# Splitting the next group's x on VectorE alone, one part per slot, with other engines for the first group's copies and another list of steps

## The chip, the cores and the metric

The kernel runs on one core of a Trainium2 chip. The metric is the device time of one execution in microseconds (us). The kernel before was run three times: median 1244.37 us, from 1243.97 to 1244.62. One more execution was taken by the hardware profiler; it took 1244.99 us.

## The reference

The inputs are x (2048 tokens of 512 values), weights of an attention with 32 query heads of 16 values that share one key head and one value head, weights of a gated feed-forward network with 1376 hidden columns, and a gate vector.

```python
g = _sigmoid((x * gate_w).sum(-1, keepdims=True))
a = _A_ref(x, A_wq, A_wk, A_wv, A_wo)          # softmax(q k^T / 4) v, then wo
b = _B_ref(x, B_w_gate, B_w_up, B_w_down)      # (gelu(x w_gate) * (x w_up)) w_down
return g * a + (1 - g) * b
```

## The kernel before, in words

**Number format.** The projections and the network are computed in three passes: each float32 operand is split into a high part (rounded to the matmul's fp32r type by a cast, L198) and a low part (the remainder by a subtraction, L199), and high x high, high x low and low x high are added up in PSUM. `split` makes the two parts; `split_part` does it for one staged piece of 128x512 and then calls `fetch`, which issues the DMA of a later piece on SyncE's queue. Four staging tiles `st` hold the pieces, three of them fetched ahead. A transfer into a tile waits until the subtraction that last read it is over. Normally the cast runs on VectorE and the subtraction on GpSimd.

**Order of the work.** The tokens stand in four groups of 512. A prologue goes through the groups in the order 1, 2, 3, 0: keys, values, one block of the network, and the queries (four blocks b of L258 for each group), which go to DRAM. For the last of these, group 0, x is also copied into the layout of the main loop (`xd`, 16 copies of 64x1024, L495 to L505 of the kernel), four copies after each block b. Then come the maximum of the bounds (`pairmax`, L510 to L514, which needs the bound of the last block, L284), the shift row, and the first scores.

**The main loop** is written out as a list, `PLAN`, and played by `play`. One line is one job on TensorE: a gate job (`f:` with 24 steps F of two matmuls on 64 rows each, L550), two down jobs after every three or four gate jobs (L561; 18 or 24 F), or an output job (`w:`). H takes the two PSUM banks z and y for the job, R ends it. S and Z are scores of the attention (L796, two matmuls and an exp on ScalarE, L800, of 1024 columns); Z takes the third of the score banks, which is the one that z uses. V adds one tile of probabilities x values (L867, 8 matmuls). T and the scores that follow move the steps of the gelu on: copy out of z (L587), two operations (L590, L591), a tanh on ScalarE (L594), two operations (L597, L598; the second reads y), and a split of the result (L602, L603).

**Slots.** After every third F of a job one piece of waiting work is put on VectorE's queue (`slot`): first from `todo` (splits of weights and of x), else from `bg` (the normalization of the attention: reciprocals L833 and others). In the first half of a job with two terms lists (`pair_mm`), `todo` is passed over in late slots. A down job's result is added to `acc` from its banks at its end (L665, L667): VectorE's queue is in order, so this waits for whatever was put there before, and the next job's H, or a Z, needs the banks. When a chunk of attention ends, its bank is copied out (L810, L821).

**Change of group.** After the last gate job of a group, `queue_x` puts the next group's x, eight parts, into `todo`, two to an item: the first split normally, the second wholly on VectorE. They are done in the two down jobs that follow. There are three such changes.

Of the kernel before, what the change touches and what calls it, by code (L numbers as in the profile page):

```python
# [20 lines left out]
S = 2048  # L21
# [98 lines left out]
def mix_kernel(ctx, tc, xT, xD, wq, wo, wf, out):  # L120
# [257 lines left out]

    def queue_x(tg):
        ps = x_parts(tg)  # L380

        def two(a, b):
            split_part(a)
            split_part(b, nc.vector)

        todo.extend(lambda i=i: two(ps[i], ps[i + 1]) for i in range(0, len(ps), 2))
# [37 lines left out]
    def first_gelu(tg):  # L424
# [17 lines left out]
        def halves():  # L442
# [7 lines left out]
            else:  # L450
                for a, h in enumerate((hh, hl)):
                    nc.sync.dma_start(hs[tg - 1, a], h.bitcast(F32))

        return inner, tanh, outer, halves

    def v_rows(tg):
        nc.scalar.copy(vt[32 * tg : 32 * tg + 32], first[tg][1][RF:P])

    hold = []
    supply.pop(0)  # L460
    d_tiles(0)
    fetch()
    for ti, tg in enumerate(order):
        xh, xl = xs[tg]
# [90 lines left out]
    def pair_mm(z, y, X, Y):  # L555
        for half in range(2):
            for q in range(len(X)):
# [15 lines left out]
                if q % EVERY == EVERY - 1 and (half == 0 or q + 4 <= len(X)):  # L573
                    slot(half == 1 or q + 6 <= len(X))
# [414 lines left out]
```

## Time and profile before

| what | before |
|---|---|
| median of three runs | 1244.37 us |
| the profiled execution, its time | 1244.99 us |
| its span, first to last instruction | 1243.2 us |
| mean granted TensorE clock | 0.993 |
| TensorE busy | 1226.1 us (99%) |
| ScalarE busy | 1031.0 us (83%) |
| VectorE busy | 600.2 us (48%) |
| GpSimd busy | 229.2 us (18%) |
| DMA, mean rate | 62 GB/s |

The engines are called PE (TensorE's matmuls), PEld (its weight loads), DVE (VectorE), ACT (ScalarE), POOL (GpSimd) and SP (SyncE, which issues most DMAs; SPq is its queue). L199 is line 199 of the kernel. A row of a timeline gives the start in us from the span's start, the duration in us, the engine, line and operation, output <- input by the program's names, and how many such instructions are merged; in brackets stands how long the engine was idle before, and what ended that. A group of concurrent matmuls overlaps, so durations of single matmuls don't add up. The mean clock of a window is 1.00 where TensorE's full clock was granted throughout.

### The profile page before, as it was taken

What the parts mean: (1) busy time and instruction counts of PE and PEld (TensorE: products, weight loads), DVE (VectorE), ACT (ScalarE), POOL (GpSimd) and SP (SyncE); (2) the same over time, 40 slices, a digit from 0 to 9 for tenths busy, and PEclk for the clock granted to TensorE, in tenths of its full rate; (3) what the DMA queues carried; (4) which work ended last, traced back from release to release, by engine and by line L of the source; (5) the groups of instructions that cost most, each with busy time, mean ns of one, the idle gap of its engine ahead of it and who ended that gap; (6) DMA issues with size and microseconds to landing.
All of it is one profiled execution on the core that took longest, in us unless ns stands there. A gap on an engine that the chain in (4) does not pass through costs nothing.

```text
span 1243.2 us, 23284 instructions
## 1 busy us (share of the span) xinstructions
PE 1226.1 (99%) x9742; PEld 680.0 (55%) x9742; DVE 600.2 (48%) x856; ACT 1031.0 (83%) x1131; POOL 229.2 (18%) x196
## 2 busy tenths in 40 slices
PE   9999999999999999999999999999989999999998
PEld 7865455545455555555555555554545554555555
DVE  7884166345545145533736244533755332471543
ACT  5458998887699888898888789888869898899883
POOL 5531033021121012101222011201231000120200
PEclk9999999999899999999999999999989999999999
DMA  8641031012221111102231111201231110110100
GB/s 330 212 130 49 1 95 53 23 58 64 68 75 48 32 48 57 40 23 65 69 103 45 48 40 49 57 23 40 69 93 55 56 32 25 51 56 24 40 1 34
DMA packets 41563, 77.03 MB, mean 62 GB/s; under 512 B 5680, under 2 KB 5936, under 8 KB 41456
## 3 DMA queue, kind: packets, MB, share of 16 engines
q1 hardware_dynamic: 40912, 74.47, 19.5%
q8 instruction: 77, 1.26, 0.4%
q0 software_dynamic: 256, 0.79, 0.2%
q14 instruction: 30, 0.25, 0.1%
q10 hardware_dynamic: 288, 0.26, 0.1%
HBM read 60.56 MB, written 14.94 MB: 61 GB/s over the span
## 4 chain that ended last, share of the span: by engine, by line
PE 87%; DVE 5%; ACT 1%; DMA 0%; issue 0%; ACTq 0%; DVEq 0%
PE acc L867 36%; PE s L796 22%; PE z L550 15%; PE z L561 8%; PE y L561 4%; PE y L550 2%; DVE xl L199 1%; PE wos L538 1%; DVE xh L198 0%; ACT p L800 0%; DMA st<-xD 0%; DVE n L830 0%; DVE nz L827 0%; DVE hl L603 0%; PE u L538 0%; DVE acc L677 0%
## 5 line engine op out<-in xcount | busy, mean ns | idle before, releaser
L800 ACT ACTIVATE p<-s 128x1024 f32<-128x1024 f32 x1024 | 972.7, 1026 | 146.6 <-PE s L796 145.2
L867 PE MATMUL acc<-p,v 128*32 128x512 f32 x4096 | 487.7, 601 | 0.0
L796 PE MATMUL s<-Q,kp 51*128 51x512 f32 x2048 | 385.4, 416 | 8.1 <-DVE acc L667 7.5
L796 PEld LDWEIGHTS s<-Q,kp 51*128 51x128 f32 x2048 | 186.6, 185 | 216.7 <-ACT p L800 110.2
L199 POOL TENSOR_TENSOR gl<-st,gh 128x512 fp32r<-128x512 f32 x80 | 112.7, 1428 | 862.7 <-PE s L796 439.2
L867 PEld LDWEIGHTS acc<-p,v 128*32 128x32 f32 x4096 | 115.8, 109 | 254.2 <-issue 243.7
L550 PE MATMUL y<-xh,gh 64*128 64x512 f32 x312 | 123.1, 395 | 1.5 <-DVE gs L598 1.5
L550 PE MATMUL z<-xh,gh 64*128 64x512 f32 x312 | 123.2, 395 | 0.0
L550 PE MATMUL z<-xl,gh 64*128 64x512 f32 x312 | 122.3, 392 | 0.0
L587 DVE COPY gs<-z 128x512 f32<-128x512 f32 x39 | 26.4, 676 | 198.6 <-PE y L550 189.8
L550 PE MATMUL y<-xl,gh 64*128 64x512 f32 x312 | 122.2, 392 | 0.0
L550 PE MATMUL y<-xh,gl 64*128 64x512 f32 x312 | 121.8, 390 | 0.0
L550 PE MATMUL z<-xh,gl 64*128 64x512 f32 x312 | 121.8, 390 | 0.0
L561 PE MATMUL y<-dh,hh 64*128 64x512 f32 x176 | 71.2, 405 | 0.2 <-DVE acc L667 0.2
L561 PE MATMUL z<-dh,hh 64*128 64x512 f32 x176 | 71.2, 405 | 0.0
L199 POOL TENSOR_TENSOR dl<-st,dh 128x512 fp32r<-128x512 f32 x44 | 64.7, 1473 | 24.4 <-DVE dh L198 20.9
L561 PE MATMUL y<-dl,hh 64*128 64x512 f32 x176 | 69.1, 393 | 0.0
L561 PE MATMUL z<-dl,hh 64*128 64x512 f32 x176 | 69.1, 392 | 0.0
L561 PE MATMUL z<-dh,hl 64*128 64x512 f32 x176 | 68.9, 391 | 0.0
L561 PE MATMUL y<-dh,hl 64*128 64x512 f32 x176 | 68.8, 391 | 0.0
L550 PEld LDWEIGHTS z<-xl,gh 64*128 64x128 f32 x312 | 58.4, 187 | 9.8
L550 PEld LDWEIGHTS z<-xh,gl 64*128 64x128 f32 x312 | 57.5, 184 | 10.6
(180 smaller groups left out, 1529.6 us busy)
## 6 DMA issues: line engine op xcount, KB each, us to landing
st<-wf SPq DMA_DIRECT2D x125, 256.0 KB
scr<-q SPq DMA_DIRECT2D x16, 512.0 KB
Q<-scr SPq DMA_DIRECT2D x64, 128.0 KB
st<-xD SPq DMA_DIRECT2D x24, 256.0 KB
Q<-scr SPq DMA_DIRECT2D x64, 64.0 KB
out<-acc SPq DMA_DIRECT2D x16, 256.0 KB
xr<-xT SPq DMA_DIRECT2D x6, 512.0 KB
xr<-xT SPq DMA_DIRECT2D x4, 256.0 KB
```

The lines of the kernel that those rows point to most:

```text
L199: eng_l.tensor_sub(lo, src, hi)
L538: nc.tensor.matmul(ps, a, b, start=(first and q == 0), stop=(last and q == len(terms) - 1), skip_group_check=True)
L550: nc.tensor.matmul(ps, a[rs], b[rs], start=(q == 0), stop=(q == len(X) - 1), skip_group_check=True)
L561: mm = nc.tensor.matmul(ps, a[rs], b[rs], start=(half == 0 and q == 0), stop=(half == 1 and q == len(X) - 1), skip_group_check=True)
L587: nc.vector.tensor_copy(gs, g)
L796: nc.tensor.matmul(ps[:, j * TG : (j + 1) * TG], kp[rs, kc * P : (kc + 1) * P], Q[u][rs, pr], start=True, stop=True)
L800: nc.scalar.activation(pb[s][:, pr], ps, AF.Exp, bias=0.0, scale=SCALE)
L867: nc.tensor.matmul(accp[u][32 * j : 32 * j + 32], vt[:, kc], pb[s][:, j // 2, (j % 2) * TG : (j % 2 + 1) * TG], start=(kc == 0), stop=(kc ...
```

## The change

1. `queue_x` makes an item of each part, and each part is split wholly on VectorE. Slots that would pass over `todo` take a part of x all the same.
2. The 16 copies of the first group's x were shared out as 4 on ScalarE, 4 on VectorE and 8 on GpSimd, four after each block b. Now ScalarE and GpSimd have two each after the first and the second block, ScalarE two after the third, and the last six run on ScalarE after the copy of v's rows (`v_rows`). VectorE has none, GpSimd four.
3. `PLAN` is another list: 70 lines of the same kinds in the same order, with the same number of each step.

```diff
 PLAN = [
     "t: S2",
...
-    "f: H F3 S F3 S F3 S F3 S F3 S F3 S F3 S F3 R S V S Z T S V6 S",
-    "f: H F3 S F3 S F3 S F3 S F3 S F3 S F4 S F2 R S V3 T S Z S V2 S",
-    "f: H F3 S F6 S2 F6 S F3 R S V Z S2 V3 S",
+    "f: H F3 S F3 S F3 S F3 S F3 S F3 S F3 S F3 R S V Z S T S V4 S Z S V2 S",
+    "f: H F3 S F3 S F3 S F3 S F3 S F3 S F6 R S2 V4 T S Z S V2 S",
+    "f: H F3 S F6 S2 F7 S F2 R S V2 S",
...
+    on_vector = []
+
     def queue_x(tg):
-        ps = x_parts(tg)
-
-        def two(a, b):
-            split_part(a)
-            split_part(b, nc.vector)
-
-        todo.extend(lambda i=i: two(ps[i], ps[i + 1]) for i in range(0, len(ps), 2))
+        for p in x_parts(tg):
+            on_vector.append(lambda p=p: split_part(p, nc.vector))
+            todo.append(on_vector[-1])
...
+    spread = []
+
+    def copy_x(eng):
+        dst, src = spread.pop(0)
+        nc.scalar.copy(dst, src) if eng == "a" else nc.gpsimd.tensor_copy(dst, src)
...
-                for eng in ("a", "d", "p", "p"):
-                    dst, src = spread.pop(0)
-                    if eng == "a":
-                        nc.scalar.copy(dst, src)
-                    else:
-                        (nc.vector if eng == "d" else nc.gpsimd).tensor_copy(dst, src)
+                for eng in ("apap", "apap", "aa", "")[b]:
+                    copy_x(eng)
...
-                    slot(half == 1 or q + 6 <= len(X))
+                    slot(half == 1 or q + 6 <= len(X) or (todo and todo[0] in on_vector))
...
     v_rows(0)
+    while spread:
+        copy_x("a")
     for step in steps[2:]:
         step()
```

The three pairs of lines shown are jobs 12 to 14 of the list: the last two gate jobs of the first group and the down job that follows. The matching jobs at the second change of group read now `... R S V S Z T S V4 Z S2 V2 S` (gate) and `H F3 S F6 S2 F9 R S2 V2 Z S2 V2 S` (down), at the third `... R S V3 T S2 Z V3 S` and `H F2 S F4 S F3 S F2 S F3 S F3 S F R V S Z S V2 S`.

VectorE's queue at the first change of group, before, from the end of the gelu (`hl`) to the first drain of the down job (`acc<-z`); `xh` and `xl` are x's high and low parts:

```order
L603 TENSOR_TENSOR hl_3384<-gs_3348,hh_3383 128x512
L198 CAST xh_3416<-st 128x512 x2
L199 TENSOR_TENSOR xl_3418<-st,xh_3416 128x512
L833 RECIPROCAL nz_2866<-n_3227 128x128 x2
L198 CAST xh_3416<-st 128x512 x2
L199 TENSOR_TENSOR xl_3418<-st,xh_3416 128x512
L198 CAST xh_3417<-st 128x512 x2
L199 TENSOR_TENSOR xl_3419<-st,xh_3417 128x512
L667 SCALAR_TENSOR_TENSOR acc_1405<-z,gc,acc_1405 128x512
```

The same stretch now; three more pairs of cast and subtraction stand in the place left out:

```order
L603 TENSOR_TENSOR hl_3401<-gs_3357,hh_3400 128x512
L198 CAST xh_3433<-st 128x512
L199 TENSOR_TENSOR xl_3435<-st,xh_3433 128x512
...
L198 CAST xh_3434<-st 128x512
L199 TENSOR_TENSOR xl_3436<-st,xh_3434 128x512
L667 SCALAR_TENSOR_TENSOR acc_1434<-z,gc,acc_1434 128x512
```

Before, six parts and two reciprocals stood ahead of the drain, with three subtractions of the six on GpSimd; now it is five parts with all their subtractions. At the other two changes of group five parts stand there too.

ScalarE's queue at the end of the prologue, before: `q` is the queries' cast of blocks 1 to 3, `xh` and `xl` the copies, `vt` v's rows, `hh` the last cast of the gelu. After it come the branch on the flag and the first exp.

```order
L503 COPY xh_674<-xh_539 64x2x512
L290 CAST q_2_716<-pq_2_703 128x512
L503 COPY xl_675<-xl_540 64x2x512
L290 CAST q_3_745<-pq_3_732 128x512
L503 COPY xl_676<-xl_540 64x2x512
L457 COPY vt<-uf_630 32x512
L446 CAST hh_777<-gsf_648 96x512
```

And now:

```order
L461 COPY xh_674<-xh_539 64x2x512 x2
L290 CAST q_2_716<-pq_2_703 128x512
L461 COPY xl_675<-xl_540 64x2x512 x2
L290 CAST q_3_743<-pq_3_730 128x512
L455 COPY vt<-uf_630 32x512
L461 COPY xl_675<-xl_540 64x2x512 x2
L461 COPY xl_676<-xl_540 64x2x512 x4
L444 CAST hh_777<-gsf_648 96x512
```

Each cast of q has two copies ahead of it instead of one, and six copies have come between v's rows and the gelu's cast.

VectorE's queue in the gelu of the gate job two before the first change of group, before:

```order
L591 SCALAR_TENSOR_TENSOR sq_3176<-sq_3176,gs_3175 128x512
L821 COPY n_3227<-acc_2989 128x512
L597 SCALAR_TENSOR_TENSOR sq_3176<-sq_3176,gs_3175 128x512
L598 SCALAR_TENSOR_TENSOR gs_3175<-y,sq_3176 128x512
L198 CAST gh_3244<-st 128x512
```

And now:

```order
L591 SCALAR_TENSOR_TENSOR sq_3176<-sq_3176,gs_3175 128x512
L597 SCALAR_TENSOR_TENSOR sq_3176<-sq_3176,gs_3175 128x512
L598 SCALAR_TENSOR_TENSOR gs_3175<-y,sq_3176 128x512
L602 CAST hh_3226<-gs_3175 128x512
L603 TENSOR_TENSOR hl_3227<-gs_3175,hh_3226 128x512
L823 COPY n_3247<-acc_2989 128x512
```

The copy out of the attention bank, which waits for the last V of its chunk, has moved from the middle of the gelu to behind it. In the new list no such copy stands inside any gelu.

More of the change, by code (lines that the diff above doesn't have):

```diff
@@ L497, in mix_kernel @@
                     xd_tiles(tg)
-                    spread = [(xd[tg][v][k][64 * a : 64 * a + 64, e::2], xs[tg][v][64 * e : 64 * e + 64, 2 * k : 2 * k + 2])
+                    spread[:] = [(xd[tg][v][k][64 * a : 64 * a + 64, e::2], xs[tg][v][64 * e : 64 * e + 64, 2 * k : 2 * k + 2])
                               for v in range(2) for k in range(2) for a in range(2) for e in range(2)]
-                for eng in ("a", "d", "p", "p"):
-                    dst, src = spread.pop(0)
-                    if eng == "a":
-                        nc.scalar.copy(dst, src)
-                    else:
-                        (nc.vector if eng == "d" else nc.gpsimd).tensor_copy(dst, src)
+                for eng in ("apap", "apap", "aa", "")[b]:
+                    copy_x(eng)
     def pairmax():
```

124 rows, old and new, of the table PLAN are left out of this document.

## The prediction

> **What bounds the kernel now.** I read the page first. Its busy table says that TensorE has hardly any time to spare:
>
> ```profile
> PE 1226.1 (99%) x9742; PEld 680.0 (55%) x9742; DVE 600.2 (48%) x856; ACT 1031.0 (83%) x1131; POOL 229.2 (18%) x196
> ```
>
> TensorE is busy for 1226.1 of the span's 1243.2 us. Its work is the same before and after, so a change of order can gain only where TensorE stands still or runs slowly. The view of TensorE's waits (engine and line that wait, who is waited for, total us, times, longest) names where it stands still:
>
> ```profile
> PE s L796 <- DVE acc L667: 7.5, 2, 4.5
> PE pm L510 <- DVE mm L289: 2.0, 1, 2.0
> PE y L550 <- DVE gs L598: 1.5, 1, 1.5
> PE pw L211 <- DVE kmx L212: 1.2, 1, 1.2
> ```
>
> There are three more waits, of 0.2 us each. All are for VectorE. The 1.2 us lie in the warm-up at the start, which stays. Where it runs slowly, the view by windows shows: after the colon the window's length, then PE, PEld, DVE, ACT and POOL busy with their counts, then the granted clock. In every other 20 us of the span the clock is 1.00.
>
> ```profile
> 60.00:80.00 20.00, 18.05 (x76) 14.03 (x74) 17.59 (x27) 8.34 (x13) 9.20 (x10) 0.91 0.41 141
> 100.00:120.00 20.00, 20.00 (x172) 11.51 (x170) 5.05 (x8) 17.61 (x19) 2.88 (x3) 1.00 0.18 50
> 300.00:320.00 20.00, 17.01 (x137) 9.90 (x138) 18.01 (x25) 14.24 (x16) 5.96 (x5) 0.93 0.45 130
> 320.00:340.00 20.00, 20.00 (x152) 8.88 (x146) 6.42 (x11) 14.36 (x16) 0.60 (x2) 0.89 0.16 51
> 900.00:920.00 20.00, 15.50 (x112) 6.99 (x110) 12.72 (x20) 11.36 (x12) 5.42 (x4) 0.87 0.40 115
> 920.00:940.00 20.00, 20.00 (x168) 14.30 (x168) 5.15 (x7) 16.25 (x17) 5.49 (x4) 0.96 0.22 65
> ```
>
> So each of the three longer waits (2.0, 3.0 and 4.5 us) also costs clock: 0.09 x 20 = 1.8 us at 60 to 80, (0.07 + 0.11) x 20 = 3.6 us at 300 to 340, (0.13 + 0.04) x 20 = 3.4 us at 900 to 940. The wait of 1.5 us, near 295, costs none. Waits and clock together are the stake: about 18 us.
>
> **The first change of group (300 to 325 us).** TensorE's timeline (start, us, what; in brackets the idle time before it):
>
> ```profile
> 302.90 2.78 PE L867 MATMUL acc<-p,v 128*32 128x512 f32 x24
> 305.61 0.97 PE L796 MATMUL s<-Q,kp 51*128 51x512 f32 x6
> 308.70 0.40 PE L561 MATMUL z<-dh,hh 64*128 64x512 f32 x1
> 313.81 0.40 PE L796 MATMUL s<-Q,kp 51*128 51x512 f32 x2
> 318.19 1.65 PE L796 MATMUL s<-Q,kp 51*128 51x512 f32 x6 [2.99 <-DVE acc L667]
> 319.77 4.97 PE L867 MATMUL acc<-p,v 128*32 128x512 f32 x24
> ```
>
> The first down job ends at 313.81, and a Z score wants its bank, which VectorE drains late. The slow clock made the next 24 matmuls 4.97 us instead of 2.78 and the 6 scores 1.65 instead of 0.97: 2.9 us lost. VectorE in the same stretch:
>
> ```profile
> 308.09 0.69 DVE L603 TENSOR_TENSOR hl<-gs,hh 128x512 fp32r<-128x512 f32 x1
> 308.69 0.76 DVE L198 CAST xh<-st 128x512 fp32r<-128x512 f32 x2
> 309.49 1.67 DVE L199 TENSOR_TENSOR xl<-st,xh 128x512 fp32r<-128x512 f32 x1
> ...
> 315.84 1.63 DVE L199 TENSOR_TENSOR xl<-st,xh 128x512 fp32r<-128x512 f32 x1
> 317.40 0.74 DVE L667 SCALAR_TENSOR_TENSOR acc<-z,gc,acc 128x512 f32<-128x512 f32 x1
> ...
> 320.80 0.43 DVE L198 CAST xh<-st 128x512 fp32r<-128x512 f32 x1 [1.67 <-DMA st<-xD]
> 321.26 0.69 DVE L199 TENSOR_TENSOR xl<-st,xh 128x512 fp32r<-128x512 f32 x1
> ```
>
> and GpSimd:
>
> ```profile
> 315.61 1.32 POOL L199 TENSOR_TENSOR xl<-st,xh 128x512 fp32r<-128x512 f32 x1 [1.02 <-DVE xh L198]
> ```
>
> From 308.69, the end of the gelu, to 317.40 VectorE works without a break. The drain at 317.40 is queued behind three pairs of x's parts and two reciprocals. A subtraction takes 1.63 to 1.67 us while GpSimd subtracts the pair's other part, and 0.69 us alone (321.26).
>
> **Change, part 1: x's parts wholly on VectorE.** It removes 12 subtractions from GpSimd and adds them to VectorE. A part then costs 0.43 + 0.69 = 1.12 us, a pair 2.24; before, a pair took 0.76 + 1.67 = 2.4 us of VectorE. So VectorE is not loaded more. The bound on the other side is the row beside GpSimd: 0.43 + 1.67 = 2.10 us a part. I take 1.12, since no GpSimd work of any kind is left in that stretch. The Trainium skill's page "SBUF — State Buffer" (its terms, "shared port pair") says that VectorE and GpSimd share a pair of ports, which one holds for a full instruction while the other blocks. By that rule a subtraction that meets one of GpSimd's waits for all of it, and the upper bound of a part would be 0.43 + 1.32 + 0.69 = 2.4 us (an estimate); the row of the trace says less, 2.10.
>
> The drain of the first down job now stands behind five parts and no reciprocals. Will it be on time? The steps are counted from the end of the matmuls of the last gate job (R). In the trace R is about 302.6, a score ahead of the V at 302.90, and x starts at 308.69, R + 6.1. A score is one step, a down job's F another: 18 F and 5 S took 313.81 - 308.70 = 5.1 us, so 0.22 a step; a V is 2.78 / 3 = 0.93. A part's DMA takes 3.3 us from issue to use (below), and part 5 is issued when part 1 is done, so VectorE waits about 0.5 us for it: five parts take 6.1 us.
> - First change: the new list plays S2 V4 S Z S V2 S after R, 6.9 us, then 18 F and 4 S, 4.9: the job ends at R + 11.8. x starts at R + 6.1, five parts are done at 12.2, z's drain (0.7) at 12.9, y's at 13.6. Both banks are wanted at 11.8 + S V2 S = 14.1. To spare: 0.5.
> - Second: seven S and seven V, 8.1, then 18 F and 3 S, 4.6. The tanh stands behind three exps instead of one, so x starts near R + 7.0; z is drained by 13.8 and wanted by Z at 12.7 + S2 V2 = 15.0. To spare: 1.2.
> - Third: five S and six V, 6.7, then 18 F and 6 S, 5.3, to R + 12.0. VectorE is free at R there, so x starts near R + 5.7 (an estimate from the same rows); z is drained at 12.9 and wanted by Z after V S, at 13.1. To spare: 0.2.
>
> So the waits of 3.0 and 4.5 us go, and with them 2.9 and 3.0 us of clock (the third's 3.4 less what falls into its own idle time). The three other parts of x come in the second job, ahead of its drains, with 3.4 us of work in more than 7. For the narrow places I take 0.4 us off.
>
> **The transfers.** The third change had another cause. VectorE, TensorE and the queue on SyncE there:
>
> ```profile
> 913.48 0.43 DVE L198 CAST xh<-st 128x512 fp32r<-128x512 f32 x1 [3.92 <-DMA st<-xD]
> ```
> ```profile
> 915.35 1.22 PE L796 MATMUL s<-Q,kp 51*128 51x512 f32 x4 [4.50 <-DVE acc L667]
> ```
> ```profile
> 909.29 1.38 SPq L366 DMA_DIRECT2D st<-xD  x3
> ```
>
> A part issued at 909.29, behind eight small loads of Q, was used at 913.48, after 4.2 us; the drain stood behind it. At the first change the last part is the nearest row without such loads: issued at 317.50, used at 320.80, 3.3 us.
>
> ```profile
> 317.50 0.33 SPq L366 DMA_DIRECT2D st<-xD  x1
> ```
>
> In the changed order the last five loads of x stand together at all three changes, with Q's loads ahead of them or behind, and those ahead fall into the gate job before. Hence 3.3, with 4.2 as the other end.
>
> **Part 2: the first group's copies (head).**
>
> ```profile
> 62.23 5.03 POOL L505 CAST xl<-xl 64x1024 fp32r<-64x1024 f32 x4
> ```
> ```profile
> 63.85 1.41 DVE L433 SCALAR_TENSOR_TENSOR sqf<-sqf,gsf 96x512 f32<-96x512 f32 x1
> 67.81 1.04 DVE L505 CAST xh<-xh 64x1024 fp32r<-64x1024 f32 x1
> 72.85 0.68 DVE L284 TENSOR_REDUCE qmx<-pq 128x1 f32<-128x512 f32 x1
> ```
> ```profile
> 68.67 1.05 ACT L503 CAST xl<-xl 64x1024 fp32r<-64x1024 f32 x1
> 83.84 1.03 ACT L800 ACTIVATE p<-s 128x1024 f32<-128x1024 f32 x1 [6.21 <-PE s L796]
> ```
> ```profile
> 71.45 0.39 PE L420 MATMUL uf<-xh,gl 128*128 128x512 f32 x1
> ```
>
> TensorE comes to the pair maximum (L510) near 71.8 and waits 2.0 us, for VectorE's bound at 72.85 is late. Three copies ahead of it (at 1.04 us or less, some 2.2 together) go. L433 and the operation after it lose about 0.7 each, as the subtraction does: the four GpSimd copies that stay end where the first row above begins. VectorE could then do the bound at 72.85 - 2.2 - 1.3 = 69.3; its bank is full at about 69.8 (eight matmuls of 0.23 ahead of 71.45, and one's 0.39 on top of the last). But ScalarE's copies double: from L433's result near 64.5, a tanh (0.6, an estimate) and twice two copies and a cast of q (2.5 each) reach 70.1, and VectorE's subtraction and bound after it 71.4. TensorE comes at 71.8: no wait, and no slow clock after it. What is late next is ScalarE. TensorE's last matmul for v's rows ends near 73, the copy of these rows at 73.6, six more copies of 1.0 at 79.5, a last cast of the gelu at 80.1. The first exp, now at 83.84, could start then, 3.7 us earlier, just as much as everything moves up. I take 0.3 off for it; were ScalarE 1 to 3 us later, as much of the gain would go.
>
> **Part 3: the list.** The steps are the same in number; runs of V go from 214 to 213, and changes from F to V from 10 to 6. At some 0.1 us a joint that is nothing, to half a us either way. One thing it moves is plain: before, VectorE's copy of the attention bank stood inside the gelu.
>
> ```profile
> 293.17 0.69 DVE L821 COPY n<-acc 128x512 f32<-128x512 f32 x1 [5.32 <-PE acc L867]
> ```
> ```profile
> 295.24 0.49 PE L550 MATMUL y<-xh,gh 64*128 64x512 f32 x1 [1.48 <-DVE gs L598]
> ```
>
> Now no copy of that kind stands inside any gelu, and the 1.5 us go. New waits elsewhere cost between nothing (the old list shows 0.6 us outside the places above) and perhaps two of this 1.5 us kind, 3 us; I take nothing, the nearer row.
>
> **The sum.** Head 2.0 + 1.8 - 0.3 = 3.5. Gelu 1.5. First change 3.0 + 2.9 = 5.9, third 4.5 + 3.0 = 7.5, second 0.2 (one of the small waits), less 0.4. Together 18.2 us. The profiled execution took 1244.99 us (span 1243.2 and 1.8 around it), which gives 1226.8; it is 0.6 above the median of 1244.37, so against the median I forecast **1226.2 us**.
>
> **The rivals.**
> - *One change still waits* (0.12). The third has 0.2 us to spare. A wait of 3 us and its 3 us of clock would return: about 1232. For it speaks the 4.2 us transfer; against it, the order of the loads.
> - *The head gives nothing* (0.09). ScalarE's six copies take the place of VectorE's three: 1226.2 + 3.5 = 1229.7. Against: 83.84 leaves it 6.21 us idle.
> - *The slow clock does not come from the waits* (0.05). Then 1.8 + 2.9 us remain and the time is 1230.9. Against: each slow stretch follows a wait of at least 2.0 us and none stands elsewhere. The Trainium skill's page "TensorE: Matmul & The Clock Gate", part 1 (the HAM clock gate), lets the clock drop after an idle window of about 3.4 us, which waits of 2.0 and 3.0 us would not fill; the trace says that they suffice.
> - *Slower: the transfers set the pace* (0.06). Parts 4 and 5 each arrive 3.9 us late, as at 913.48. VectorE stands still with the drain behind it: 7.8 us, less the 0.5 already counted and 0.5, 1.2 and 0.2 to spare, so waits of 6.8, 6.1 and 7.1 us and 3 us of clock each, 29 us where there were 13.6 (with the second change's 0.2). With the head and gelu gains of 5.0 that is 1244.4 + 15 - 5 = 1254 us. It decides for slower from about 3.2 us of wait at each change.
> - *No change* (0.06). Either a part still costs 2.10 us: five are 4.9 us later, the waits of 3.9, 3.2 and 4.2 us with 9 us of clock are 20 instead of 13.6, and the head and gelu pay for it, 1246; or the new list has waits of its own, 0.27 us in each of 69 jobs: 1244. The 0.6 us of the old list speak against the second.
>
> **How the numbers follow.** The forecast has 0.62. A measurement of this kernel can tell about 0.2% (2.5 us) from no change. Faster: 0.62 + 0.12 + 0.09 + 0.05 = 0.88; same 0.05; slower 0.07 (the transfers, and part of the 1246 case). The range reaches down to 1223.9, where nothing is lost at ScalarE and the narrow places (0.7), joints save half a us and the clock's two terms are the windows' 3.6 and 3.4 us (1.1 more), and up to 1233.5, which takes in the three rivals on the fast side.
>
> **What would show it.** Right: TensorE's waits fall from 12.9 us to 2 or 3, no L667 among those over 1 us, clock 1.00 in all windows but the start, subtractions of x at 0.69, first exp near 80. Wrong: VectorE idle for a transfer ahead of a drain, subtractions near 1.6, TensorE waiting for ScalarE after the head, or small waits spread over many jobs.

## The result, and the profile after it

| | before | after |
|---|---|---|
| median of six runs, us | 1244.06 (1242.99 to 1244.62) | 1231.61 (1230.61 to 1231.97) |
| ratio after to before | | 0.990, 95% interval 0.9888 to 0.9913 |
| profiled execution, us (its span) | 1244.99 (1243.2) | 1231.97 (1230.1) |

The change gains 12.5 us; 18.2 were forecast. The time lies inside the range of 1223.9 to 1233.5 us. The waits of TensorE in the profile after, all that there are (engine, line and tile that wait, who is waited for; total us, times, longest):

```profile
PE y L550 <- DVE gs L587: 2.0, 1, 2.0
PE s L798 <- ACT p L802: 1.6, 1, 1.6
PE pw L211 <- DVE kmx L212: 1.2, 1, 1.2
PE pm L510 <- DVE mm L289: 0.6, 1, 0.6
```

The 12.8 us of before are 5.4. The drains (L667) and the gelu's wait at 295 us are gone altogether, and the wait for the pair maximum (pm) fell from 2.0 to 0.6, where none was forecast. New are the first two rows, 2.0 us and 1.6. Both lie in one place, as the windows show (length, then PE, PEld, DVE, ACT, POOL busy, then the granted clock, the DMA's share and its GB/s):

```profile
60.00:80.00 20.00, 19.23 (x87) 15.21 (x86) 13.02 (x26) 15.87 (x20) 3.10 (x5) 1.00 0.41 142
80.00:100.00 20.00, 16.24 (x112) 9.46 (x110) 13.70 (x21) 14.35 (x18) 5.64 (x4) 0.91 0.26 75
300.00:320.00 20.00, 20.00 (x171) 11.75 (x170) 17.64 (x30) 16.02 (x18) 1.98 (x2) 1.00 0.42 137
900.00:920.00 20.00, 20.00 (x168) 10.57 (x168) 14.15 (x25) 16.86 (x19) 0.00 (x0) 1.00 0.43 137
```

At the first and the third change of group TensorE no longer stands still and its clock is 1.00, where 0.93 and 0.87 stood before. From 80 to 100 us, right behind the head, it stands still for 3.8 us, and the clock there is 0.91, worth 0.09 x 20 = 1.8 us more.

**The main loop did what the prediction said.** VectorE at the first change, from the first of the last five parts of x to the drains:

```profile
309.58 0.42 DVE L198 CAST xh<-st 128x512 fp32r<-128x512 f32 x1
310.03 0.69 DVE L199 TENSOR_TENSOR xl<-st,xh 128x512 fp32r<-128x512 f32 x1
...
314.29 0.69 DVE L199 TENSOR_TENSOR xl<-st,xh 128x512 fp32r<-128x512 f32 x1
316.06 0.75 DVE L667 SCALAR_TENSOR_TENSOR acc<-z,gc,acc 128x512 f32<-128x512 f32 x1 [1.08 <-PE z L561]
```

A subtraction takes 0.69 us, a part 1.06, and no part waits for its load: five take 314.98 - 309.58 = 5.4 us. The bracket in the last row says who waits now: VectorE, 1.08 us, for TensorE to finish z. At the second and third change VectorE waits likewise:

```profile
611.17 0.75 DVE L667 SCALAR_TENSOR_TENSOR acc<-z,gc,acc 128x512 f32<-128x512 f32 x1 [1.59 <-PE z L561]
912.73 0.75 DVE L667 SCALAR_TENSOR_TENSOR acc<-z,gc,acc 128x512 f32<-128x512 f32 x1 [1.97 <-PE z L561]
```

**The head did not.** From 73 to 88 us, in order of time over four engines: ScalarE's copies of x and the cast behind them, GpSimd, VectorE, TensorE, then ScalarE and TensorE once more.

```profile
74.18 6.37 ACT L461 CAST xl<-xl 64x1024 fp32r<-64x1024 f32 x6
80.57 0.62 ACT L444 CAST hh<-gsf 96x512 fp32r<-96x512 f32 x1
81.22 1.02 ACT L802 ACTIVATE p<-s 128x1024 f32<-128x1024 f32 x1
```
```profile
81.27 1.26 POOL L445 TENSOR_TENSOR hl<-gsf,hh 96x512 fp32r<-96x512 f32 x1 [18.00 <-ACT hh L444]
```
```profile
82.56 0.69 DVE L587 COPY gs<-g 128x512 f32<-128x512 f32 x1 [4.41 <-POOL hl L445]
```
```profile
80.34 0.74 PE L798 MATMUL s<-Q,kp 51*128 51x512 f32 x4
83.31 0.50 PE L550 MATMUL y<-xh,gh 64*128 64x512 f32 x1 [2.01 <-DVE gs L587]
87.52 0.50 PE L798 MATMUL s<-Q,kp 51*128 51x512 f32 x2 [1.61 <-ACT p L802]
```
```profile
85.93 0.63 ACT L594 ACTIVATE sq<-sq 128x512 f32<-128x512 f32 x1 [3.69 <-DVE sq L591]
```

Each bracket names the row above it. The six late copies keep the first gelu's cast hh until 80.57. GpSimd needs hh to subtract hl and still reads gsf for it. The tile gs has one buffer for gsf and for the next gelu's gs, so VectorE can copy g out of its bank only at 82.56. TensorE's y takes over that bank (tag pf) and waits 2.0 us. The next gelu's tanh is late with it, at 85.93; it stands in ScalarE's queue ahead of the second exp, so the scores wait 1.6 us too. The first score had come at 80.34, against 83.15 before; those 2.8 us were given back at once, and more: TensorE's first V (`acc<-p,v`) starts at 94.18, against 91.57 before, 2.6 us later.

### The profile page after: what moved, and what is told of

It reads as the page before. It is cut to its first block, busy times and chain, and to the rows that moved or that the text cites. A ratio compares the mean times of both kernels' runs of the same rounds, so it can differ in the third digit from the quotient of the medians.

```text
span 1230.1 us, 23272 instructions
## 1 busy us (share of the span) xinstructions
PE 1220.3 (99%) x9742; PEld 678.2 (55%) x9742; DVE 593.7 (48%) x864; ACT 1040.6 (85%) x1139; POOL 207.8 (17%) x180
## 4 chain that ended last, share of the span: by engine, by line
PE 92%; issue 2%; DVE 2%; DMA 1%; POOL 1%; ACT 1%; POOLq 0%; ACTq 0%
PE acc L869 38%; PE s L798 23%; PE z L550 14%; PE z L561 9%; PE y L561 4%; PE y L550 3%; PE wos L538 1%; DMA scr<-q 1%; DMA wqs<-wq 1%; POOL xh L461 0%; DMA st<-wf 0%; ACT p L802 0%; POOL hl L445 0%; POOL gl L199 0%; DVE kp L267 0%
```

## The experiments

Each time stands against the kernel before as it ran beside it. Its median was 1243.3 us beside the kernels cast first, late copies on GpSimd, old copies and new copies; 1243.77 beside gsf with its own memory, new split, new list and x's subtractions on GpSimd; 1243.72 beside the last three of the table. The intervals of the ratios are up to 0.0017 either way, about 2 us, because the kernel before spread over 1.6 to 4.3 us from run to run. The changed kernels are mostly steadier (0.1 to 2.6 us from the lowest to the highest, over four runs or more), so differences between them are read from their medians, and differences below 1 us are not read at all.

| kernel | median, us | ratio to before | us below before |
|---|---|---|---|
| changed kernel | 1231.61 | 0.990 (0.9888 to 0.9913) | 12.5 |
| cast first | 1227.7 | 0.9871 (0.9856 to 0.9886) | 15.6 |
| late copies on GpSimd | 1227.53 | 0.9872 (0.9857 to 0.9887) | 15.8 |
| changed, old copies | 1228.61 | 0.9879 (0.9864 to 0.9894) | 14.7 |
| before, new copies | 1245.79 | 1.0019 (1.001 to 1.0028) | -2.5 |
| gsf with its own memory | 1228.23 | 0.9878 (0.9862 to 0.9895) | 15.5 |
| before, new split | 1230.59 | 0.9899 (0.9883 to 0.9916) | 13.2 |
| before, new list | 1231.08 | 0.99 (0.9883 to 0.9916) | 12.7 |
| changed, x's subtractions on GpSimd | 1232.38 | 0.9906 (0.9889 to 0.9922) | 11.4 |
| before, new split, no late slots | 1232.5 | 0.9913 (0.9899 to 0.9926) | 11.2 |
| the same, subtractions on GpSimd | 1235.22 | 0.9932 (0.9919 to 0.9946) | 8.5 |
| cast first, copies dealt anew | 1226.28 | 0.986 (0.9845 to 0.9875) | 17.4 |

### The head: is it the six copies, and by which link?

The theory was the chain shown above. Its rival was that ScalarE simply has too much to copy ahead of the exps.

**The cast first.**

```
-    while spread:
-        copy_x("a")
     for step in steps[2:]:
         step()
+    while spread:
+        copy_x("a")
```

> The gelu's last steps (outer product and halves) come ahead of ScalarE's six late copies; nothing else changes. Theory (the six copies hold up the cast hh, with it GpSimd's hl, the one gs buffer, VectorE's copy of g and so y's bank): the waits of 2.0 us (y for gs) and 1.6 us (s for p) and the 1.7 us of half clock go, 1231.6 - 5.3 = about 1226.3 us, although ScalarE does the same twelve copies and the first exp starts no earlier than 81. Rival (it is ScalarE's total of copies ahead of the exps that holds TensorE): the wait only changes its name to s for p, within 1 us of 1231.6.

1227.7 us, 15.6 below before and 3.1 more than the changed kernel gains. TensorE's waits there, but for the warm-up's 1.2 us,

```profile
...
PE s L798 <- ACT p L802: 1.0, 2, 0.7
PE pm L510 <- DVE mm L289: 0.6, 1, 0.6
```

and ScalarE's first exp:

```profile
82.08 1.02 ACT L802 ACTIVATE p<-s 128x1024 f32<-128x1024 f32 x1
```

The wait of y is gone, the waits for p are 1.0 us instead of 1.6, and the clock is 1.00 throughout. ScalarE's work is the same and its first exp is even later, 82.08 instead of 81.22. So the total of the copies is not what held TensorE; where the cast stood among them was. The gain over the changed kernel is 3.1 us where 5.3 were expected; of the 2.2 us that are missing, 1.0 are the wait for p that stayed.

**The late copies on GpSimd** (`copy_x("p")` instead of `copy_x("a")`, in the same place).

> The last six copies go to GpSimd, which stands idle from about 63 to 81, instead of ScalarE. Theory: the cast hh comes near 75 and y no longer waits, about 1226.3 us as with the cast first; VectorE's head operations that meet a GpSimd copy may lose some 0.7 each, but TensorE's wait for the pair maximum stays near 0.6. Rival (ScalarE's total): gains as well, and more than the cast first does. Second rival (contention of VectorE with GpSimd decides in the head): the pair maximum's wait comes back to 2 us with 1.8 of clock, 1229 or more.

1227.53 us, level with the cast first. GpSimd does the six copies from 62.22 to 69.80 us:

```profile
62.22 7.58 POOL L461 CAST xl<-xl 64x1024 fp32r<-64x1024 f32 x6
```

The wait for the pair maximum rises from 0.6 to 1.5 us, more than halfway to the second rival's 2.0:

```profile
73.32 0.38 PE L510 MATMUL pm<-ident,mm 128*1 128x128 f32 x2 [1.50 <-DVE mm L289]
```

So GpSimd's copies do cost VectorE something in the head, but 1.5 us of waiting took no clock, and the waits for p fall to 0.3 in exchange.

**gsf with memory of its own.**

```
-        gs = cp.tile([P, TG], F32, tag="gs", name=f"gsf{tg}", bufs=1)
+        gs = pp.tile([P, TG], F32, tag="gsf", name=f"gsf{tg}", bufs=1)
```

> The changed kernel, with the six late copies ahead of the cast hh as it has them; only the first gelu's tile gsf gets memory of its own, so that VectorE's copy of g no longer waits for GpSimd's hl. Theory (the link that holds TensorE is the one gs buffer): y no longer waits, VectorE copies g near 78.8 us; about the time of the kernel with the cast first, 15.6 us below the kernel before, though hh still comes at 80.6. Rival (the late cast holds up something else, the tanh or the exps behind it on ScalarE): s for p waits instead, about 12.5 us below the kernel before, as the changed kernel.

(pp is a pool of the head, free again when the main loop begins.) 1228.23 us, 15.5 below before. Here the six copies still stand ahead of the cast, which comes at 80.53; only VectorE's copy of g no longer has to wait for GpSimd to be done with gsf:

```profile
78.73 0.69 DVE L587 COPY gs<-g 128x512 f32<-128x512 f32 x1 [0.63 <-DVEq L736]
```

The wait of y is gone. This shows the link: one shared buffer made a late cast on ScalarE into a late bank on TensorE. The scores still wait 1.4 us for p, and the first exp itself now waits for GpSimd's hl, which it does not do in the changed kernel:

```profile
82.54 1.02 ACT L802 ACTIVATE p<-s 128x1024 f32<-128x1024 f32 x1 [1.40 <-POOL hl L445]
```

The edit brought this wait with it; how stays open.

**The head of before, with the rest new; and the new copies alone on the kernel before.** The first takes back the copies (one on ScalarE, one on VectorE, two on GpSimd behind each of the four q blocks); the second has the new copies with the old list and the old split.

> The changed kernel with the copies of before (one ScalarE, one VectorE, two GpSimd after each of the four q blocks); new list and new split of x stay. Theory (the head of after loses 5.9 us in waits and clock, that of before 3.8): 1231.6 - 2.1 = about 1229.5 us. Rival (the head gained as forecast and the list or split has the loss): 1231.6 + 3.5 = 1235.

> The kernel before with the new spread of copies alone (old list, old split of x). Theory: 1244.1 + 2.1 = about 1246.2 us, slower than before. Rival (the head gained as forecast): 1244.1 - 3.5 = 1240.6.

1228.61 and 1245.79 us. The new copies lose 14.7 - 12.5 = 2.2 us by the first and 2.5 us by the second, whose interval alone is 1.2 to 3.5 us. So part 2 of the change makes the kernel slower by some 2.4 us; all the gain, and 2.4 us besides, comes from the list and the split.

The size is less sure than the sign. By the start of TensorE's first V in the profiles, the new copies cost 94.18 - 91.28 = 2.9 us with the new list and split, and 92.60 - 91.57 = 1.0 us with the old. One reason is seen: behind the old copies' wait for the pair maximum the clock fell to 0.91 in the profile of before and not at all in that of the changed kernel with the old copies. Another is that the kernel before with the new copies has no wait of 1.6 us for p.

### The main loop: the list or the split?

**Each alone, with the copies of before.**

> The kernel before with the new split of x alone (one part a slot, subtractions on VectorE, x also in the late slots of a pair); old list and old copies. Theory (three pairs beside GpSimd and two reciprocals made the first change's drain late, the loads of x behind Q's loads the third's): the first change's wait and clock shrink to 1 us at most, the third's stay: 5 to 6 us below the kernel before, about 1238.5. Rival (the split alone carries the main loop): 14 us below, 1230.

> The kernel before with the new list of steps alone; old split of x (pairs, half of the subtractions on GpSimd) and old copies. Theory: the list takes away the gelu's 1.5 us and most of the third change's 7.5 us (the loads stand otherwise) and of the first change's 5.9 (no reciprocals ahead of the drain, six V instead of the bank's release so early), but the drain still stands behind three pairs of 2.4 us, so a wait of 0.5 to 2 us is left at one or two changes: 9 to 13 us below the kernel before, 1231 to 1235. Rival (without the split the list gives nothing but the gelu): 2 us below, 1242.

1230.59 us for the split alone, 13.2 below; 1231.08 for the list alone, 12.7 below. Together they gave 14.7. Here the theory fell on one side: the split alone was to leave the third change's wait, and it took all of them. Its waits:

```profile
PE pm L514 <- DVE mm L289: 1.9, 1, 1.9
PE y L554 <- DVE gs L602: 1.5, 1, 1.5
...
```

No drain among them; the gelu's 1.5 us, which only the list removes, is still there. Why the third change is mended too is seen on VectorE and on the queue of SyncE of the split alone:

```profile
896.71 0.42 DVE L198 CAST xh<-st 128x512 fp32r<-128x512 f32 x1
897.16 0.69 DVE L199 TENSOR_TENSOR xl<-st,xh 128x512 fp32r<-128x512 f32 x1
...
902.03 0.74 DVE L671 SCALAR_TENSOR_TENSOR acc<-z,gc,acc 128x512 f32<-128x512 f32 x1
```
```profile
897.88 1.39 SPq L366 DMA_DIRECT2D st<-xD  x2
899.32 0.43 SPq L391 DMA_DIRECT2D Q<-scr  x1
...
902.83 1.99 SPq L366 DMA_DIRECT2D st<-xD  x2
```

(A row of SPq marked x2 merges two loads that are issued one after the other.) The first part frees its buffer at 897.8, 1.1 us after it starts, and the second as long after that; a load of x is issued each time, at 897.88 and 898.94, both ahead of Q's loads at 899.32. Five parts run through without a wait, and the drain follows at 902.03. The two loads behind Q's belong to parts behind the drain. Before, one load went out ahead of Q's (at 905.41) and three behind, from 909.29 on. The first of these three was for the sixth part, and the third pair put that part ahead of the drain. So the transfer was not late by the list's order alone: done in pairs, x puts a sixth part ahead of the drain and leaves its load behind Q's. With single parts the sixth part stands behind the drain, and its load ahead of Q's as well; these runs don't tell which of the two is enough.

The list alone still does its parts in pairs, with three pairs and two reciprocals ahead of the drain. VectorE at its first change

```profile
306.94 0.76 DVE L198 CAST xh<-st 128x512 fp32r<-128x512 f32 x2
307.74 1.66 DVE L199 TENSOR_TENSOR xl<-st,xh 128x512 fp32r<-128x512 f32 x1
...
315.67 0.74 DVE L667 SCALAR_TENSOR_TENSOR acc<-z,gc,acc 128x512 f32<-128x512 f32 x1
```

and TensorE there:

```profile
316.46 0.49 PE L561 MATMUL z<-dh,hh 64*128 64x512 f32 x1 [0.55 <-DVE acc L667]
```

From the first part to the drain it is 315.67 - 306.94 = 8.7 us, just as long as before (317.40 - 308.69 = 8.7). But TensorE comes for the bank 316.46 - 0.55 - 306.94 = 9.0 us after the first part, where before it came after 318.19 - 2.99 - 308.69 = 6.5: the new list puts more other work ahead of it. It waits 0.55 us, too little to touch the clock. Either half of the change is enough for the long waits, which is why they do not add up.

**What of the split counts?** First x's subtractions were put on GpSimd in the changed kernel (`split_part(p)` for `split_part(p, nc.vector)`). Then, on the kernel before with the new split, the rule that x may use the last slots of a pair was taken out (`or (todo and todo[0] in on_vector)` deleted); then that with the subtractions on GpSimd as well.

> The changed kernel with x one part a slot as now, but every subtraction of x on GpSimd instead of VectorE. Theory (VectorE has 1.1 us or more to spare at each drain, and five casts at 0.4 with the subtractions beside them are no longer than five parts at 1.06): the same time as the changed kernel within 1 us, 12.5 us below the kernel before. Rival (a VectorE free of GpSimd is what the main loop needs): drains late by 1 us or more, waits for L667 come back, 3 us or more above the changed kernel.

> The split alone (old list, old copies), without its rule that x may also use the last slots of a pair: one part a slot, subtractions on VectorE, otherwise as before. Theory (one part a slot frees a load's buffer after 1.06 us instead of after a pair, so that two loads of x stand ahead of Q's loads and five parts end before the job does): the waits for L667 stay away without the rule, 13.2 us below the kernel before as with it, within 1 us. Rival (the extra slots matter, since they bring x's parts out of the next job): 3 us or more of it are lost.

> As the split alone without the late slots, and with every subtraction of x on GpSimd: of the change only one part a slot is left. Theory (it is one part a slot, not VectorE, that counts): 12 to 13 us below the kernel before. Rival (the buffers, freed after GpSimd's 1.3 us, come too late for the loads ahead of Q's at the third change): 4 to 6 us above the split alone, with a wait of 2 to 4 us for L667 at one change.

1232.38 us with GpSimd's subtractions, 11.4 below before where the changed kernel is 12.5 below: the same within what the runs can tell. TensorE waits for no drain in it; its profile has one new wait, 0.8 us near 10 us, in the prologue, which the edit does not touch. That VectorE does the subtractions is not what counts while the late slots are there.

Without the late slots 1232.5 us, 2.0 less gained than with them, and 1235.22 with GpSimd's subtractions, 4.7 less. Neither guess was right. The drains stay on time in both; but only two or three parts stand ahead of a drain here instead of five, so these two kernels don't show whether five would be on time. Instead a wait for the copy of z at a gelu's start (gs, L591) appears or grows. In the kernel without the late slots, and then in the one with GpSimd's subtractions as well:

```profile
PE s L800 <- DVE gs L591: 1.7, 2, 1.5
```
```profile
PE s L800 <- DVE gs L591: 2.6, 2, 2.4
```

VectorE from 333 to 343 us in the latter, then TensorE and the window behind it:

```profile
333.48 0.75 DVE L198 CAST xh<-st 128x512 fp32r<-128x512 f32 x2
334.14 2.95 DVE L198 CAST gh<-st 128x512 fp32r<-128x512 f32 x2
339.50 0.43 DVE L198 CAST dh<-st 128x512 fp32r<-128x512 f32 x1 [2.41 <-DMA st<-wf]
...
343.30 0.68 DVE L591 COPY gs<-z 128x512 f32<-128x512 f32 x1
```
```profile
344.04 0.99 PE L800 MATMUL s<-Q,kp 51*128 51x512 f32 x6 [2.38 <-DVE gs L591]
```
```profile
340.00:360.00 20.00, 17.62 (x136) 9.03 (x134) 9.77 (x13) 14.66 (x16) 6.70 (x5) 0.91 0.38 107
```

Without the late slots the last two parts of x (the first row) slip past the down jobs into the next gate job. The weights' parts come later for it, VectorE waits for their loads, and the gelu's copy of z stands behind them. The wait of TensorE is 1.5 us with the subtractions on VectorE, and 2.4 us, with 0.09 x 20 = 1.8 us of clock, with those on GpSimd, where VectorE's wait for one load is 2.41 us. So the late slots are worth 2.0 us, and without them VectorE's subtractions 2.7, but at the next gelu, not at the drain that the prediction looked at.

### The version that the experiments point to

The cast first, and the copies dealt out so that none stands ahead of something that is waited for:

```
...
-                for eng in ("apap", "apap", "aa", "")[b]:
+                for eng in ("addpp", "app", "aa", "")[b]:
...
-    while spread:
-        copy_x("a")
     for step in steps[2:]:
         step()
+    for eng in "daaaaa":
+        copy_x(eng)
```

("d" is VectorE, "a" ScalarE, "p" GpSimd; `copy_x` takes "d" as well now.)

> The changed kernel with the cast first and the copies dealt out anew: after block 0 ScalarE one, VectorE two, GpSimd two; after block 1 one and two; after block 2 ScalarE two; behind the gelu's last step VectorE one and ScalarE five. Theory: each q cast comes 1 us earlier on ScalarE, VectorE's two copies fill a gap of 1.4 us, so the wait of 0.6 for the pair maximum goes; the first exp starts at 81.0 instead of 82.1, so the waits of 1.0 for p go: 1.6 us below the kernel with the cast first, 17.2 below the kernel before (ratio 0.9862). Rival (VectorE's extra copies come ahead of the bound, or GpSimd's fifth copy slows the gelu's products): the wait for the pair maximum stays or grows to 1.5, no better than 15.6 below.

1226.28 us (1226.22 to 1226.33), 17.4 below before, ratio 0.986, where 17.2 was expected. Its waits, all of them:

```profile
PE pw L211 <- DVE kmx L212: 1.2, 1, 1.2
PE s L798 <- ACT p L802: 0.8, 1, 0.8
```

VectorE's two early copies (0.69 us each) fill the gap ahead of the second bound, and the pair maximum has no wait left, as expected. The wait for p was to go as well, and 0.8 us of it stayed; that the time came so close is in part luck.

## Why the prediction was right, and where it was not

**The stake**, put at about 18 us, is near what can be had: the best version here gains 17.4. By the prediction's own rows it is larger: the four waits of 1.5 to 4.5 us and the three slow stretches come to 11.0 + 8.8 = 19.8.

**The main loop, 14.7 of the 18.2 us.** The changed kernel with the old copies gains 14.7 us. The terms stand: the first change's and the third's waits with their clock, and the gelu's 1.5. The kernel with the split alone shows them one by one, since it has the list of before. TensorE starts the same V at 302.81 us in it and at 302.90 before, then at 601.43 and 607.44, at 893.25 and 900.02, at 914.83 and 929.28: the three changes give 5.9, 0.8 and 7.7 us, where 5.9, 0.2 and 7.5 were forecast.

A part costs 1.06 us where 1.12 was taken, the lower bound. The five last loads stand together, as forecast; the row merges them, and from 906.53 on one is issued as each part ends:

```profile
901.93 8.12 SPq L366 DMA_DIRECT2D st<-xD  x5
```

The 0.5 us of waiting for the fifth part's load did not come. At the first change that load is issued at 310.75 and the part starts at 313.84, so 3.1 us were enough. The prediction's own figures give no wait either: the load lands 1.12 + 3.3 = 4.4 us after x starts, and four parts take 4.5.

The narrow places were a little wider than the steps gave. VectorE is done with five parts early and waits 1.08, 1.59 and 1.97 us for TensorE ahead of the first drain. From the end of the drain to TensorE's next use of the bank there are 0.9, 1.4 and 0.5 us, where 0.5, 1.2 and 0.2 were forecast. (At the third change the prediction has z drained at 12.9; its own steps, the job's end at 12.0 and 0.7 for the drain, give 12.7.) The 0.4 us taken off for them was not lost.

"No copy of that kind stands inside any gelu" does not hold for the new list as it ran: one copy out of the attention bank, at 576.01 us, stands between L598 and L602 of a gelu and waits 1.86 us for the last V. It stands behind the read of y, and TensorE waits for nothing there.

What the prediction did not see is that list and split do the same thing twice: it wrote of the new list's steps and the new split's parts as one, and either of them alone gives 12.7 or 13.2.

**The head, forecast at 3.5 us, measured at -2.4.** This is the step that failed, and with 5.9 us it is the whole shortfall (18.2 - 12.5 = 5.7). Its first half is right in the main: the slow clock behind the pair maximum is gone and TensorE came to the first score 2.8 us earlier, though not 3.7: the last bound ended at 72.2 instead of 71.4, and 0.6 us of the wait were left. Its second half was: "What is late next is ScalarE ... a last cast of the gelu at 80.1. The first exp, now at 83.84, could start then". ScalarE's queue was read rightly but for a us: the cast ended at 81.19 and the exp started at 81.22. But the prediction followed the late cast only down its own engine, to the exp, and took 0.3 us off. It did not ask who else waits for that cast. GpSimd's hl did, and by the shared buffer VectorE's copy of g, and by the bank TensorE's y, and by the tanh the second exp. The trace of before held the rows for it: the same chain ran there, with the cast at 77.02, early enough to cost nothing. The rival "the head gives nothing" named ScalarE's copies as the cause, but priced them at no loss; the measured case lies 2.4 us beyond it. That the time is inside the range all the same is luck: the room up to 1233.5 was left for another rival, a change that still waits (about 1232), and that one did not come.

**The rivals.** No change of group waits any more. The transfers do not set the pace: VectorE waits for no load ahead of a drain in the changed kernel. The new list has no waits of its own in the main loop. The slow clock comes from the waits: in the kernel with the cast first, where no wait is longer than 1.2 us, it is 1.00 in every window up to 1220 us, and in the changed kernel it is 0.91 only behind the 2.0 and 1.6 us. The price of the rival that denied this was too low: with the third change's 3.0 us of clock, which the sum counts too, 7.7 us remain and not 4.7, 1233.9 instead of 1230.9. "A part still costs 2.10" was answered by 0.69 in the row of the subtraction.

**The signs.** Of those for "right", the drains and the 0.69 came. TensorE's waits came to 5.4 us instead of 2 or 3, the clock is 0.91 from 80 to 100 us, and one sign of "wrong" was there: TensorE waiting for ScalarE after the head.

## What to carry to other kernels

When work is put on an engine's queue ahead of an instruction, list everyone who waits for that instruction, and go on through each buffer that its readers hold, until an engine is reached that has time to spare; the first thing late on the same engine is only one branch. A cast that others wait for goes ahead of copies that nobody waits for yet. Two halves of a change can each remove the same wait, so a gain is assigned to one of them only after each was run alone.

## What the runs showed of the hardware

**A wait near 2 us may or may not cost clock.** The wait for the pair maximum was 1.9 to 2.0 us in the kernel before and in the four kernels that were built on it and kept its head, and the clock was 0.91 in the window from 60 to 80 us each time. In the changed kernel with the old copies it was 1.98 us and the clock stayed at 1.00, in this window and the next:

```profile
60.00:80.00 20.00, 17.69 (x80) 13.88 (x79) 17.54 (x30) 8.36 (x13) 9.71 (x10) 1.00 0.41 140
```

Waits of 1.5 us cost none (the gelu's, and the pair maximum's with the late copies on GpSimd); the one of 2.4 us cost 1.8 us of clock, and y's wait of 2.0 us with the new copies alone as much. The Trainium skill's page "TensorE: Matmul & The Clock Gate", part 1, has the clock gate watch a free-running window of about 3.4 us. The slow stretch of the changed kernel agrees with that length; the first row is at its beginning, the last one the first behind it:

```profile
88.55 0.58 PE L798 MATMUL s<-Q,kp 51*128 51x512 f32 x2
...
91.50 0.62 PE L550 MATMUL z<-xh,gl 64*128 64x512 f32 x1
...
92.20 0.39 PE L550 MATMUL y<-xh,gh 64*128 64x512 f32 x1
```

From about 88.6 to 92.1 us a matmul takes 0.62 instead of 0.39 us, some 3.5 us long. A free-running window would also explain why one wait of 2.0 us costs clock and another does not, by how it falls on the window's edge; that was not tried. By its table an idle window is needed for the drop, and these runs show that a wait of 1.9 to 2.4 us can be enough.

**VectorE beside GpSimd.** With x's subtractions on GpSimd in the changed kernel, four of VectorE's casts take 3.62 us, where one takes 0.42 alone:

```profile
310.55 3.62 DVE L198 CAST xh<-st 128x512 fp32r<-128x512 f32 x4
```

The first two, ahead of GpSimd's first subtraction at 311.10, take 0.76 us together; the other two, beside two subtractions (311.10 to 313.88), take 2.95, about 1.5 each. Two reciprocals in the kernel with no late slots and with the subtractions on GpSimd, beside one of these (309.24 to 310.53), keep their 0.9 us:

```profile
309.03 1.75 DVE L837 RECIPROCAL nz<-n 128x128 f32<-128x128 f32 x2
```

So not every operation of VectorE is held up by GpSimd. The Trainium skill's page "SBUF — State Buffer" ("shared port pair") says that the loser of the pair blocks fully for the other's instruction; the casts agree, with 1.5 us beside a subtraction of 1.4, and the reciprocals do not show it.
